# An earlier and more regular attention schedule beside the weight products, with four heads to a row half

## The chip, the cores and the metric

The kernel runs on one core of one Trainium2 chip. What counts is the device time of one execution, in microseconds. TensorE (PE) multiplies, with PEld its weight loads; VectorE (DVE), ScalarE (ACT) and GpSimd (POOL) do the elementwise work; SP, the sync engine, issues most DMAs. Each engine works through its own instructions in the order in which they were written, and waits on semaphores where an operand or a buffer is not there.

## The reference

Chunked attention over 4 batches, 8 heads, 768 positions of 64 values: each chunk of 32 queries sees 8 memory keys and the 56 keys around it (16 to the left, 32 own, 8 to the right). Its output, 3072 tokens of 512 values, goes through two gated layers:

```
scores = scale * q_c @ k_full.T ; a = softmax(scores) ; out_c = a @ v_full
x = ((x @ w1) * (x @ w2)) @ w3 @ w_out          # widths 1024, 1024, 512
y = ((x @ w_a) * (x @ w_b)) @ moe2_w_out        # widths 1536, 512
```

## The kernel before

**Weights' phase.** Since `w3 @ w_out` does not depend on the tokens, the kernel multiplies those two first (L548 to L583): two halves of 32 products of 128x512 in full fp32, eight steps of the inner sum for each of four PSUM banks. Products 1 to 24 of a half go step by step over the four banks, then each bank gets its steps 7 and 8 together. After a bank's last step `w_evict` (L543) copies it out with ACT and takes the rest with DVE; the second half needs the banks of the first. In the trace a product is two MATMUL instructions with the output `wps`.

**Weights.** They come as 64-bit floats. `w_load` (L339) issues a tile from SP if one of its buffers is free; `w_scale` (L355) passes it twice through ACT, `w_bits` (L364) sums on DVE. `w_tick` (L393) moves this pipe by one stage per tile and then calls `w_load` until no buffer is free. The plan has 12 tiles of 1 MB for the weights' phase (`w3a`, `w3b`, together `raw2` and `w_f`), then 16 of 0.5 MB for the first layer (`w12`, `raw64`), which take two ticks more (L403, L397) to become a high and a low half. The calls of `w_tick` in the phase are placed by hand.

**Attention.** It is cut into 16 units of 192 tokens with all eight heads (two groups of 96 queries). Each has stages: `a_k` and `a_q` load keys and queries, `a_keys` copies the keys into windows on DVE, `a_scores` multiplies on PE (`sc`), `a_max` and `a_exp` (16 activations, four of them in each of four stages) make exponentials, `a_norm` divides (DVE sums, POOL products, two stages), `a_trans` transposes on PE (`pt`), `a_pt` copies with ACT (`p`), `a_v` loads values, `a_pv` multiplies on PE (`xp`), `a_x` splits the result into the high and low part of the tokens' `xt`. `BASE` (L269) gives a unit's first slot, the table at L279 the slot of each stage behind it; `attn_slot` (L302) runs the next slot. Raw keys, queries, windows, values, `sc`, and the PSUM tile shared by `pt` and `xp` have one buffer each. Three units fill the first tile of 512 tokens.

**First layer.** For each of six tiles of 512 tokens, `ab_step` does for eight `m` a product A and B of 12 fp32r matmuls each (`psA`, `psB`, L595), then 96 matmuls `psY` with the product of the weights' phase. After each such half `between` (L620) calls `w_tick` while there are tiles in the pipe, and as many slots as bring the attention evenly to `NEED` (L299), the slot by which a token tile's units must be done. `xt` of tile 0 needs units 0 to 2. After six tiles the second layer runs with seven products per block (`seven`, L825); the change does not touch it.

Of the kernel before, what the change touches and what calls it, by code (L numbers as in the profile page):

```python
# [13 lines left out]
P = 128  # L14
# [31 lines left out]
def tile_attention_moe(  # L46
# [44 lines left out]


    ks, qs, scs, soft, pts, p2s, xps = ({} for _ in range(7))
    v = att.tile([P, NE * 2, NC, 2 * D], F32, tag="v", bufs=1, name="v")
    kw = att.tile([P, NH, NC, KEYS], F32, tag="kw", bufs=1, name="kw")
    xt = {}

# [6 lines left out]
    def rows(r):  # L104
        return slice(D * r, D * r + D)

    def new_batch(u):
        return NE * u % NG == 0

    def a_k(u):  # L110
        if u >= NA:
            return
        k = ks[u] = att.tile([P, NE * 2, 2 * KW], F32, tag="kraw", bufs=1, name="kraw")
        for r in range(2):
            src = kt[2 * NE * u : 2 * NE * u + 2 * NE, 0:D, 2 * r : 2 * r + 2, :]
            nc.sync.dma_start(out=k[rows(r)], in_=src.rearrange("a d h k -> d a (h k)"))

    def a_q(u):
        if u >= NA:
            return  # L120
        q = qs[u] = att.tile([P, NE * 2, 2 * GQ], F32, tag="q", bufs=1, name="q")
        for r in range(2):
            src = qt[2 * NE * u : 2 * NE * u + 2 * NE, :, 2 * r : 2 * r + 2, :]
            nc.sync.dma_start(out=q[rows(r)], in_=src.rearrange("a d h q -> d a (h q)"))

    def a_v(u):
        if u >= NA:
            return
        for r in range(2):
            src = vw[2 * NE * u : 2 * NE * u + 2 * NE, :, 2 * D * r : 2 * D * r + 2 * D]  # L130
            src = src.rearrange("a k d -> k a d")
            for c in range(NC):
                k0 = NMEM + CHUNK * c
                if new_batch(u):
                    nc.sync.dma_start(out=v[D * r : D * r + NMEM, :, c, :], in_=src[0:NMEM])
                nc.sync.dma_start(
                    out=v[D * r + NMEM : D * r + D, :, c, :], in_=src[k0 : k0 + KEYS - NMEM]
                )

    def a_keys(u):  # L140
        if u >= NA:
            return
        k = ks.pop(u).rearrange("p a (h k) -> p (a h) k", h=2)
        p, a, e = k.ap
        win = bass.AP(
            k.tensor, k.offset + NMEM * e[0], [p, a, [CHUNK * e[0], NC], [e[0], KEYS - NMEM]]
        )
        nc.vector.tensor_copy(kw[:, :, :, NMEM:], win)
        if new_batch(u):
            nc.vector.tensor_copy(  # L150
                kw[:, :, :, 0:NMEM], k[:, :, None, 0:NMEM].to_broadcast([P, NH, NC, NMEM])
            )

    def a_scores(u):
        q = qs.pop(u).rearrange("p a (h c q) -> p (a h) c q", h=2, c=NC)
# [75 lines left out]
    def a_pv(u):  # L231
        p2 = p2s.pop(u)
        xp = psa.tile([P, 2, 512], F32, tag="px", name="xp")
        xp = xps[u] = xp[:, :, : 2 * NE * GQ].rearrange("p r (a t) -> p a r t", a=2)
        for e in range(NE):
            for a in range(2):
                for c in range(NC):
                    q0 = CHUNK * c
                    for i in range(2):
                        for r in range(2):  # L240
                            h = r ^ i
                            mm(
                                xp[rows(h), a, r, GQ * e + q0 : GQ * e + q0 + CHUNK],
                                v[rows(r), 2 * e + a, c, rows(h)],
                                p2[rows(r), e, 2 * a + h, q0 : q0 + CHUNK],
                                True,
                                True,
                            )

    def a_x(u):  # L250
        xp = xps.pop(u)
        n = NE * GQ
        t0 = n * u
        cuts = [t0, t0 + n]
        if t0 // TT != (t0 + n - 1) // TT:
            cuts.insert(1, (t0 + n - 1) // TT * TT)
        parts = []
        for c0, c1 in zip(cuts, cuts[1:]):
            ti = c0 // TT
            if ti not in xt:  # L260
                xt[ti] = xpool.tile([P, 2, KD, TT], F32R, tag="xt", name="xt")
            x = xt[ti].rearrange("p l (a r) t -> p l a r t", a=2)
# [12 lines left out]

    for u in range(NA):
        early = u < UA
        t = 6 if early else 5
        for s, stage_of in (  # L279
            (t, a_trans),  # L280
            (t + early, a_pt),
            (t + 1 + early, a_pv),
            (t + 1 + early, lambda u: a_v(u + 1)),
            (0, a_scores),
            (1, a_max),
            (2, a_norm(0)),
            (3, a_norm(1)),
            (1, a_exp(0)),
            (1, a_exp(1)),
            (2, a_exp(2)),  # L290
            (2, a_exp(3)),
            (t + 2 + early, a_x),
            (1, lambda u: a_q(u + 1)),
        ):
# [4 lines left out]
    NEED = [BASE[-(-TT * (i + 1) // (NE * GQ)) - 1] + 8 + 2 * (i == 0) for i in range(NT1)]  # L299
    acount = [0]  # L300

    def attn_slot(n=1):  # L302
# [17 lines left out]
    NW0 = max(i for i, x in enumerate(plan) if x[0] == "w3b") + 1  # L320
    wraw = []
    nload = [0]

    turn = {tag: [0, 0] for tag in BUFS}
    live = {tag: [0, 0] for tag in BUFS}
# [224 lines left out]
    for half in range(2):  # L550
        banks = [psd.tile([P, 512], F32, tag="d", name="wps") for _ in range(4)]
        for k, m in order:
            mm(
                banks[m],
                w3k[8 * half + k].bitcast(F32)[:, P * m : P * m + P],
                wo_f[k].bitcast(F32),
                k == 0,
                k == 7,
            )
            if k < 6 and m % 2 == 0 or k == 6:  # L560
                continue

            if k == 7 and m > 0:
                w_evict(half, m - 1)
            if half == 0:
                if m == 1 and k < 6:
                    w_tick()
                if (k, m) == (1, 3):
                    a_k(0)
                    a_q(0)  # L570
                if (k, m) == (4, 3):
                    a_keys(0)
                    a_v(0)
                    a_k(1)
                if k == 7 and m > 0:
                    attn_slot()
                if k == 7 and m % 2 == 1:
                    w_tick()
            else:
                attn_slot()  # L580
                if m == 3 or k == 7 and m == 1:
                    w_tick()
        w_evict(half, 3)  # L583
    del pairs["f"]
# [425 lines left out]
```

## Time and profile before

| | |
|---|---|
| median of 3 runs | 1090.26 us (1089.99 to 1092.81) |
| the profiled execution's own time | 1093.22 us |
| its span, first to last instruction | 1091.4 us |
| PE busy in the span | 1065.6 us (98%) |
| ACT, DVE, POOL busy | 441.0, 457.1, 235.0 us |
| mean granted TensorE clock | 0.99 of full speed |

Times in the trace are microseconds from the span's start. A timeline row merges like instructions that follow each other on an engine; the bracket is the idle time ahead of it and what ended it. PE's busy time contains time at a lower clock.

### The profile page before, as it was taken

The page shows a single profiled execution, that of the slowest core. Times are in us where ns is not written, and L with a number is a line of the kernel's source. Part 1 is how long each engine was busy: PE and PEld are TensorE (multiplying, and loading weights), DVE is VectorE, ACT ScalarE, POOL GpSimd, SP SyncE. Part 2 cuts the span into 40 slices and gives each one's busy share as a digit, 9 for nine tenths or more (in the row PEclk, how much of TensorE's full clock was granted, in tenths as well). Part 3 has the DMA queues.
Part 4 walks back from the last instruction along what each step waited for, and adds up shares of the span by engine and source line. Part 5 has one row for each costly group of instructions (what it writes and reads, how often), then busy time and mean ns, then how long its engine had stood idle before and what let it go on. Part 6 is the DMA issues. An engine that isn't in the chain of part 4 may idle for free.

```text
span 1091.4 us, 18538 instructions
## 1 busy us (share of the span) xinstructions
PE 1065.6 (98%) x7442; PEld 848.0 (78%) x7442; DVE 457.1 (42%) x751; ACT 441.0 (40%) x1153; POOL 235.0 (22%) x228
## 2 busy tenths in 40 slices
PE   9688999999999999999999999999999999999998
PEld 3245778888888788888878888888888888888886
DVE  5547853454444445436553443442223243222320
ACT  6656864445545535435343333232222232222220
POOL 0110230221312212202122233104222301322210
PEclk9889999999999999999999999999999999999999
DMA  9868566345464473347545455514433442443311
GB/s 331 256 143 212 158 149 188 101 132 159 128 172 142 141 190 124 103 146 260 192 156 192 174 193 197 183 63 179 159 135 135 158 160 106 161 176 136 135 39 38
DMA packets 82693, 172.03 MB, mean 158 GB/s; under 512 B 7344, under 2 KB 46000, under 8 KB 76720
## 3 DMA queue, kind: packets, MB, share of 16 engines
q1 hardware_dynamic: 72032, 104.75, 32.3%
q0 software_dynamic: 10368, 66.06, 16.6%
q8 instruction: 58, 0.95, 0.4%
q14 instruction: 27, 0.22, 0.1%
q10 hardware_dynamic: 208, 0.04, 0.0%
HBM read 137.27 MB, written 33.55 MB: 157 GB/s over the span
## 4 chain that ended last, share of the span: by engine, by line
PE 83%; ACT 2%; DVE 1%; DMA 1%; POOL 1%; issue 0%; ACTq 0%; DVEq 0%
PE ps L796 31%; PE ops L90 18%; PE psY L90 12%; PE psB L90 10%; PE psA L90 9%; PE xp L90 2%; ACT t L195 1%; PE sc L90 1%; DMA wc<-co 1%; PE pt L223 1%; POOL g L615 0%; POOL t L212 0%; DVE dec L367 0%; DVE mx L186 0%; DVE x L102 0%
## 5 line engine op out<-in xcount | busy, mean ns | idle before, releaser
L796 PE MATMUL ps<-x,w 128*128 128x512 f32 x1512 | 348.9, 389 | 0.3 <-ACT tmp L808 0.3
L796 PEld LDWEIGHTS ps<-x,w 128*128 128x128 f32 x1512 | 283.4, 188 | 60.5 <-ACT tmp L808 1.4
L813 DVE TENSOR_TENSOR tmp<-ps,tmp 128x512 f32<-128x512 f32 x108 | 74.6, 690 | 261.0 <-PE ps L796 231.0
L90 PE MATMUL psA<-xt,w 128*128 128x512 f32 x576 | 140.6, 393 | 0.0
L90 PE MATMUL psB<-xt,w 128*128 128x512 f32 x576 | 140.0, 392 | 0.0
L615 POOL TENSOR_TENSOR g<-gv,g 128x512 fp32r<-128x512 f32 x48 | 66.9, 1394 | 320.4 <-ACT g L614 293.3
L90 PE MATMUL psY<-g,wo 128*128 128x512 f32 x576 | 135.6, 392 | 0.0
L808 ACT ACTIVATE tmp<-ps 128x512 f32<-128x512 f32 x108 | 64.6, 599 | 157.8 <-PE ps L796 151.2
L90 PEld LDWEIGHTS psA<-xt,w 128*128 128x128 f32 x576 | 107.2, 188 | 23.1 <-ACT raw L362 0.5
L90 PEld LDWEIGHTS psB<-xt,w 128*128 128x128 f32 x576 | 107.2, 188 | 22.5
L90 PEld LDWEIGHTS psY<-g,wo 128*128 128x128 f32 x576 | 107.1, 188 | 22.4
L680 POOL DMA_DIRECT2D w<-wc x72 | 39.7, 552 | 373.8 <-PE ps L796 373.6
L90 PE MATMUL ops<-wo,g 128*128 128x512 f32 x504 | 118.6, 389 | 0.0
L90 PEld LDWEIGHTS ops<-wo,g 128*128 128x128 f32 x504 | 94.6, 188 | 19.7
L819 ACT ACTIVATE g<-tmp 128x512 fp32r<-128x512 f32 x66 | 40.7, 633 | 139.9 <-DVE tmp L818 139.9
L820 POOL TENSOR_TENSOR g<-tmp,g 128x512 fp32r<-128x512 f32 x66 | 84.1, 1293 | 20.4 <-ACT g L819 19.4
L195 ACT ACTIVATE t<-sc,mx 96x64 f32<-96x64 f32 x256 | 75.7, 321 | 23.5 <-DVE mx L187 23.5
L90 PE MATMUL wps<-w_f 128*128 128x512 f32 x128 | 65.9, 665 | 9.2 <-DVE wo L546 5.6
L90 PE MATMUL ops<-fo,g 128*128 128x512 f32 x288 | 68.2, 389 | 0.0
L90 PEld LDWEIGHTS ops<-fo,g 128*128 128x128 f32 x288 | 54.1, 188 | 11.2
L613 DVE TENSOR_TENSOR gv<-psB,av 128x512 f32<-128x512 f32 x48 | 33.1, 689 | 67.1 <-PE psB L90 56.1
L212 POOL TENSOR_TENSOR t<-t,sm 96x512 f32<-96x512 f32 x32 | 36.8, 1150 | 103.0 <-DVE sm L211 80.0
(65 smaller groups left out, 904.7 us busy)
## 6 DMA issues: line engine op xcount, KB each, us to landing
w<-wc POOLq DMA_DIRECT2D x36, 1024.0 KB, 6.9
w<-wc POOLq DMA_DIRECT2D x36, 768.0 KB, 5.0
wc<-co SPq DMA_DIRECT2D x84, 256.0 KB
raw<-in_wab SPq DMA_DIRECT2D x24, 512.0 KB
v<-in_vw SPq DMA_DIRECT2D x96, 112.0 KB
kraw<-in_kt SPq DMA_DIRECT2D x32, 256.0 KB
raw<-in_w SPq DMA_DIRECT2D x16, 512.0 KB
raw<-in_w3a SPq DMA_DIRECT2D x6, 1024.0 KB
```

The costliest lines, as they stand in the source:

```text
L90: nc.tensor.matmul(o, lhsT=l, rhs=r, start=first, stop=last)
L195: nc.scalar.activation(t[:, a, r, :], sc[:, r, a, :], AF.Exp, bias=mx[:, r, a : a + 1], scale=SCALE, accum_out=sm[:, a, r : r + 1],)
L212: nc.gpsimd.tensor_tensor(t, t, sm[:, :, :, None].to_broadcast([GQ, 4, 2, KEYS]), ALU.mult)
L223: nc.tensor.transpose(pt[:, a // 4, a % 4, :], t[:, a].rearrange("p r k -> p (r k)"), id_sb)
L613: nc.vector.tensor_tensor(gv, psB[:, :TT], av, ALU.mult)
L615: nc.gpsimd.tensor_tensor(g2[:, 1, :], gv, g2[:, 0, :].bitcast(F32), ALU.subtract)
L680: nc.gpsimd.dma_start(out=t[:, c0:c1].bitcast(F32), in_=src[:, c0:c1])
L796: nc.tensor.matmul(ps, lhsT=w[:, i, a, k, :], rhs=xs[i][:, b, k, :], start=first and n == 0, stop=n == 5, skip_group_check=not first,)
L808: nc.scalar.activation(z, ps, AF.Copy)
L813: nc.vector.tensor_tensor(z, ps, y, ALU.add)
L819: nc.scalar.activation(g2[:, 0, :], z, AF.Copy)
L820: nc.gpsimd.tensor_tensor(g2[:, 1, :], z, g2[:, 0, :].bitcast(F32), ALU.subtract)
```

## The change

Four things, in one edit.

1. The layout of a unit in the two row halves. Before, rows 0 to 63 held heads 0 and 1 of each four, rows 64 to 127 heads 2 and 3. Now each row half holds all four heads of one group of four. So a run of keys in memory is 2 KB instead of 1 KB, of queries 1536 bytes instead of 768, of values 1 KB instead of 512, and the three windows of values come in one DMA.
2. The slots: `BASE` starts 0, 7, 14, 23, 30, 36 and then goes on by 7; the first six units have one slot more between scores and transposes and one more before the probabilities' copy; unit 0 has all its exponentials in slot 1; queries of the next unit are loaded in the slot of the scores, raw keys of the next with the copy of the keys.
3. The weights' phase: `a_k(0)` and `a_q(0)` come after the third tick, the first slot after product 18; there are 24 slots instead of 19 (with unit 3's scores in the last), and the ticks stand elsewhere (19 before and now).
4. `w_load` issues no tile of the first layer until product 42 (`bound`).

```diff
-    v = att.tile([P, NE * 2, NC, 2 * D], F32, tag="v", bufs=1, name="v")
+    v = att.tile([P, NE, NC, 4 * D], F32, tag="v", bufs=1, name="v")
...
+    def group(src, u, r):
+        return src[2 * NE * u : 2 * NE * u + 2 * NE].rearrange("(e r) x h y -> r x e (h y)", r=2)[r]
...
-            src = kt[2 * NE * u : 2 * NE * u + 2 * NE, 0:D, 2 * r : 2 * r + 2, :]
-            nc.sync.dma_start(out=k[rows(r)], in_=src.rearrange("a d h k -> d a (h k)"))
+            nc.sync.dma_start(out=k[rows(r)], in_=group(kt[:, 0:D], u, r))
...
+                win = bass.AP(
+                    src.tensor,
+                    src.offset + NMEM * kd[0],
+                    [[kd[0], KEYS - NMEM], [CHUNK * kd[0], NC], x],
                 )
+                nc.sync.dma_start(out=v[D * r + NMEM : D * r + D, e, :, :], in_=win)
...
-    BASE = [0, 5, 9]
-    BASE += [BASE[-1] + 10 + 7 * i for i in range(NA - UA)]
+    BASE = [0, 7, 14, 23, 30, 36]
+    NX = len(BASE)
+    BASE += [BASE[-1] + 7 * i for i in range(1, NA - NX + 1)]
...
-        early = u < UA
-        t = 6 if early else 5
+        x = int(u < NX)
+        t = 5 + 2 * x
         for s, stage_of in (
-            (t, a_trans),
-            (t + early, a_pt),
-            (t + 1 + early, a_pv),
-            (t + 1 + early, lambda u: a_v(u + 1)),
+            (5 + x, a_trans),
+            (t, a_pt),
+            (t + 2, a_x),
+            (t + 1, a_pv),
+            (t + 1, lambda u: a_v(u + 1)),
             (0, a_scores),
+            (0, lambda u: a_q(u + 1)),
...
-            (2, a_exp(2)),
-            (2, a_exp(3)),
+            (1 + (u > 0), a_exp(2)),
+            (1 + (u > 0), a_exp(3)),
...
-            at(BASE[u] - 2, (a_keys, u))
-            at(BASE[u] - 1, (a_k, u + 1))
+            at(BASE[u] - 2, (a_keys, u), (a_k, u + 1))
+    at(0, (a_v, 0))
...
-        if i < len(wsrc):
+        if i < bound[0]:
...
+    a_k(0)
+    a_q(0)
...
+            g = 2 * k + m // 2 if k < 6 else 12 + m
             if half == 0:
...
+                if g == 7:
                     a_keys(0)
                     a_k(1)
+                if g >= 8:
                     attn_slot()
+                if g in (0, 2, 4, 6, 8, 9, 14):
                     w_tick()
             else:
                 attn_slot()
+                if g == 4:
+                    bound[0] = len(wsrc)
+                if g in (1, 3, 4, 5, 6, 9, 10, 11, 12):
                     w_tick()
```

PE in the weights' phase, before (each `sc`, `pt`, `xp` row is one unit's):

```order
L90 MATMUL wps<-w_f 128x512 x28
L90 MATMUL sc<-kw,q 32x64 x48
L90 MATMUL wps<-w_f 128x512 x10
L90 MATMUL sc<-kw,q 32x64 x48
L90 MATMUL wps<-w_f 128x512 x2
L223 MATMUL pt<-id_sb,t 128x96 x8
L90 MATMUL wps<-w_f 128x512 x4
L90 MATMUL xp<-p_451,v 64x32 x48
```

PE in the same phase with the change, and its end at the first `psA`:

```order
L90 MATMUL wps<-w_f 128x512 x18
L90 MATMUL sc<-kw,q 32x64 x48
L90 MATMUL wps<-w_f 128x512 x12
L227 MATMUL pt<-id_sb,t 128x96 x8
L90 MATMUL wps<-w_f 128x512 x2
L90 MATMUL sc<-kw,q 32x64 x48
L90 MATMUL wps<-w_f 128x512 x2
L90 MATMUL xp<-p_354,v 64x32 x48
...
L90 MATMUL wps<-w_f 128x512 x2
L90 MATMUL sc<-kw,q 32x64 x48
L90 MATMUL psA<-xt,w_693 128x512 x12
```

The first scores moved from product 28 to 18, the first transposes and probability-by-value products forward by 10 and 8 products, and unit 3's scores to the front of `psA`.

ACT from the seventh weight tile on, before (`raw` rows scale a tile, `wo` rows evict a bank, `t` rows are exponentials):

```order
L361 ACTIVATE raw_183<-raw_183 128x1024
L362 ACTIVATE raw_183<-raw_183 128x1024
L545 ACTIVATE wo<-wps 128x512
L361 ACTIVATE raw_193<-raw_193 128x1024
L362 ACTIVATE raw_193<-raw_193 128x1024
L545 ACTIVATE wo<-wps 128x512
L195 ACTIVATE t,sm<-sc,mx 96x64 x8
L545 ACTIVATE wo<-wps 128x512
L195 ACTIVATE t,sm<-sc,mx 96x64 x8
```

ACT with the change (`raw_172` is the eighth tile, `raw_183` the ninth, `raw_277` the eleventh, `raw_523` the first of the first layer):

```order
L370 ACTIVATE raw_172<-raw_172 128x1024
L371 ACTIVATE raw_172<-raw_172 128x1024
L199 ACTIVATE t,sm<-sc,mx 96x64 x16
L370 ACTIVATE raw_183<-raw_183 128x1024
L371 ACTIVATE raw_183<-raw_183 128x1024
L557 ACTIVATE wo<-wps 128x512 x2
...
L370 ACTIVATE raw_277<-raw_277 128x1024
L371 ACTIVATE raw_277<-raw_277 128x1024
...
L370 ACTIVATE raw_523<-raw_523 128x512
L371 ACTIVATE raw_523<-raw_523 128x512
L233 ACTIVATE p_544<-pt 128x768
```

All 16 exponentials of unit 0 stand ahead of the evictions now, and the copy of unit 1's probabilities (`p_544`) stands behind the first tile of the first layer.

SP's queue with the change, from the sixth tile (`raw_143`) and, lower, from unit 2's keys on:

```order
L355 DMA raw_143<-in_w3a 128x2048
L118 DMA kraw<-in_kt 64x2x512 x2
L125 DMA q<-in_qt 64x2x384 x2
L355 DMA raw_162<-in_w3a 128x2048
L355 DMA raw_172<-in_w3a 128x2048
...
L118 DMA kraw<-in_kt 64x2x512 x2
L125 DMA q<-in_qt 64x2x384 x2
L142 DMA v<-in_vw 56x3x256 x4
L118 DMA kraw<-in_kt 64x2x512 x2
L355 DMA raw_523<-in_w 128x1024
```

Before, the first keys and queries stood behind the eighth tile, and the first-layer tiles ahead of unit 1's queries.

## Rows read from the trace of the kernel before

**Rows 1.** The page, part 2: tenths in 40 slices of the span, granted clock below.

```profile
PE   9688999999999999999999999999999999999998
PEclk9889999999999999999999999999999999999999
```

**Rows 2.** Windows, first weight product to first psA: busy us by engine, clock, DMA share, GB/s.

```profile
8.58:99.14 90.56, 75.75 (x729) 36.02 (x729) 49.10 (x74) 57.49 (x153) 7.67 (x6) 0.89 0.81 229
```

**Rows 3.** Timeline of PE, weights' phase: start, us, what, [idle before, releaser].

```profile
8.58 21.98 PE L90 MATMUL wps<-w_f 128*128 128x512 f32 x50
34.11 4.54 PE L90 MATMUL wps<-w_f 128*128 128x512 f32 x6 [3.55 <-DVE w_f L367]
38.58 1.19 PE L90 MATMUL sc<-kw,q 64*32 64x64 f32 x96
...
47.25 1.37 PE L90 MATMUL wps<-w_f 128*128 128x512 f32 x2 [2.13 <-DVE wo L546]
52.10 5.49 PE L90 MATMUL wps<-w_f 128*128 128x512 f32 x6 [3.49 <-DVE wo L546]
59.96 0.27 PE L90 MATMUL sc<-kw,q 64*32 64x64 f32 x2 [2.37 <-DMA q<-in_qt]
...
77.58 0.82 PE L223 MATMUL pt<-id_sb,t 96*128 96x96 f32 x8
...
82.88 1.60 PE L90 MATMUL xp<-p,v 64*64 64x32 f32 x96 [1.00 <-ACT p L229]
...
94.83 1.59 PE L90 MATMUL xp<-p,v 64*64 64x32 f32 x78 [0.54 <-DMA v<-in_vw]
```

**Rows 4.** Timeline of DVE, weights' phase.

```profile
31.06 0.86 DVE L148 COPY kw<-kraw 128x1344 f32<-128x1344 f32 x1 [4.32 <-DMA kraw<-in_kt]
...
32.83 1.23 DVE L367 CUSTOM_DVE_ANT_0 w_f<-raw,w_f 128x2048 uint16<-128x2048 uint16 x1
...
46.50 0.69 DVE L546 TENSOR_TENSOR wo<-wps,wo 128x512 fp32r<-128x512 f32 x1 [3.06 <-ACT wo L545]
```

**Rows 5.** Timeline of ACT, weights' phase.

```profile
28.59 1.15 ACT L361 ACTIVATE raw<-raw 128x1024 f32<-128x1024 f32 x1 [3.10 <-DMA raw<-in_w3a]
...
43.53 0.31 ACT L195 ACTIVATE t<-sc,mx 96x64 f32<-96x64 f32 x1 [2.59 <-DVE mx L187]
...
45.87 0.60 ACT L545 ACTIVATE wo<-wps 128x512 fp32r<-128x512 f32 x1
...
86.23 0.68 ACT L361 ACTIVATE raw<-raw 128x512 f32<-128x512 f32 x1 [0.33 <-DMA raw<-in_w]
```

**Rows 6.** Timeline of SP's queue: start and length of DMA issues.

```profile
11.75 6.74 SPq L346 DMA_DIRECT2D raw<-in_w3a  x3
18.54 1.48 SPq L116 DMA_DIRECT2D kraw<-in_kt  x2
...
47.78 1.74 SPq L124 DMA_DIRECT2D q<-in_qt  x2
...
78.47 6.97 SPq L346 DMA_DIRECT2D raw<-in_w  x2
```

**Rows 7.** Windows of 2 us, columns as in rows 2.

```profile
14.00:16.00 2.00, 1.92 (x5) 0.68 (x4) 1.43 (x3) 1.71 (x3) 0.00 (x0) 1.00 1.02 430
24.00:26.00 2.00, 2.00 (x6) 0.91 (x5) 1.18 (x2) 1.49 (x2) 0.00 (x0) 1.00 1.00 158
34.00:36.00 2.00, 1.89 (x3) 0.86 (x4) 0.06 (x1) 0.70 (x1) 0.00 (x0) 0.59 1.05 438
82.00:84.00 2.00, 1.12 (x76) 1.12 (x80) 1.77 (x4) 1.93 (x6) 1.29 (x1) 1.00 0.86 220
```

**Rows 8.** Timeline of PE in the first token tile: the rows with idle time.

```profile
122.13 1.60 PE L90 MATMUL xp<-p,v 64*64 64x32 f32 x96 [1.23 <-ACT p L229]
143.85 0.55 PE L223 MATMUL pt<-id_sb,t 96*128 96x96 f32 x4 [1.87 <-POOL t L212]
170.57 1.60 PE L90 MATMUL xp<-p,v 64*64 64x32 f32 x96 [0.50 <-ACT p L229]
```

More of the change, by code (lines that the diff above doesn't have):

```diff
@@ L112, in a_k @@
             return
-        k = ks[u] = att.tile([P, NE * 2, 2 * KW], F32, tag="kraw", bufs=1, name="kraw")
+        k = ks[u] = att.tile([P, NE, 4 * KW], F32, tag="kraw", bufs=1, name="kraw")
         for r in range(2):
-            src = kt[2 * NE * u : 2 * NE * u + 2 * NE, 0:D, 2 * r : 2 * r + 2, :]
-            nc.sync.dma_start(out=k[rows(r)], in_=src.rearrange("a d h k -> d a (h k)"))
+            nc.sync.dma_start(out=k[rows(r)], in_=group(kt[:, 0:D], u, r))
     def a_q(u):
@@ L120, in a_q @@
             return
-        q = qs[u] = att.tile([P, NE * 2, 2 * GQ], F32, tag="q", bufs=1, name="q")
+        q = qs[u] = att.tile([P, NE, 4 * GQ], F32, tag="q", bufs=1, name="q")
         for r in range(2):
-            src = qt[2 * NE * u : 2 * NE * u + 2 * NE, :, 2 * r : 2 * r + 2, :]
-            nc.sync.dma_start(out=q[rows(r)], in_=src.rearrange("a d h q -> d a (h q)"))
+            nc.sync.dma_start(out=q[rows(r)], in_=group(qt, u, r))
     def a_v(u):
@@ L129, in a_v @@
         for r in range(2):
[L130 to L133, printed above, removed]
+            for e in range(NE):
+                src = vw[2 * NE * u + 2 * e + r]
+                kd, x = src.ap
                 if new_batch(u):
-                    nc.sync.dma_start(out=v[D * r : D * r + NMEM, :, c, :], in_=src[0:NMEM])
-                nc.sync.dma_start(
-                    out=v[D * r + NMEM : D * r + D, :, c, :], in_=src[k0 : k0 + KEYS - NMEM]
+                    for c in range(NC):
+                        nc.sync.dma_start(out=v[D * r : D * r + NMEM, e, c, :], in_=src[0:NMEM])
+                win = bass.AP(
+                    src.tensor,
+                    src.offset + NMEM * kd[0],
+                    [[kd[0], KEYS - NMEM], [CHUNK * kd[0], NC], x],
                 )
+                nc.sync.dma_start(out=v[D * r + NMEM : D * r + D, e, :, :], in_=win)
     def a_keys(u):
@@ L142, in a_keys @@
             return
-        k = ks.pop(u).rearrange("p a (h k) -> p (a h) k", h=2)
+        k = ks.pop(u).rearrange("p e (h k) -> p (e h) k", h=4)
         p, a, e = k.ap
@@ L154, in a_scores @@
     def a_scores(u):
-        q = qs.pop(u).rearrange("p a (h c q) -> p (a h) c q", h=2, c=NC)
+        q = qs.pop(u).rearrange("p e (h c q) -> p (e h) c q", h=4, c=NC)
         sc = psa.tile([GQ, 2, 512], F32, tag="sc", name="sc")
@@ L233, in a_pv @@
         xp = psa.tile([P, 2, 512], F32, tag="px", name="xp")
-        xp = xps[u] = xp[:, :, : 2 * NE * GQ].rearrange("p r (a t) -> p a r t", a=2)
+        xp = xps[u] = xp[:, :, : 2 * NE * GQ].rearrange("p r (a t) -> p r a t", a=2)
         for e in range(NE):
@@ L242, in a_pv @@
                             mm(
-                                xp[rows(h), a, r, GQ * e + q0 : GQ * e + q0 + CHUNK],
-                                v[rows(r), 2 * e + a, c, rows(h)],
+                                xp[rows(h), r, a, GQ * e + q0 : GQ * e + q0 + CHUNK],
+                                v[rows(r), e, c, rows(2 * a + h)],
                                 p2[rows(r), e, 2 * a + h, q0 : q0 + CHUNK],
@@ L261, in a_x @@
                 xt[ti] = xpool.tile([P, 2, KD, TT], F32R, tag="xt", name="xt")
-            x = xt[ti].rearrange("p l (a r) t -> p l a r t", a=2)
+            x = xt[ti].rearrange("p l (r a) t -> p l r a t", r=2)
             parts.append((xp[..., c0 - t0 : c1 - t0], x[..., c0 - TT * ti : c1 - TT * ti]))
@@ L289, in tile_attention_moe @@
             (1, a_exp(1)),
-            (2, a_exp(2)),
-            (2, a_exp(3)),
-            (t + 2 + early, a_x),
-            (1, lambda u: a_q(u + 1)),
+            (1 + (u > 0), a_exp(2)),
+            (1 + (u > 0), a_exp(3)),
         ):
@@ L296, in tile_attention_moe @@
         if u > 0:
-            at(BASE[u] - 2, (a_keys, u))
-            at(BASE[u] - 1, (a_k, u + 1))
-    NEED = [BASE[-(-TT * (i + 1) // (NE * GQ)) - 1] + 8 + 2 * (i == 0) for i in range(NT1)]
+            at(BASE[u] - 2, (a_keys, u), (a_k, u + 1))
+    at(0, (a_v, 0))
+    NEED = []
+    for i in range(NT1):
+        u = -(-TT * (i + 1) // (NE * GQ)) - 1
+        NEED.append(BASE[u] + 8 + 2 * (u < NX))
     acount = [0]
@@ L322, in tile_attention_moe @@
     nload = [0]
+    bound = [NW0]
     turn = {tag: [0, 0] for tag in BUFS}
@@ L564, in tile_attention_moe @@
                 w_evict(half, m - 1)
+            g = 2 * k + m // 2 if k < 6 else 12 + m
             if half == 0:
[L566 to L571, printed above, removed]
+                if g == 7:
                     a_keys(0)
-                    a_v(0)
                     a_k(1)
-                if k == 7 and m > 0:
+                if g >= 8:
                     attn_slot()
-                if k == 7 and m % 2 == 1:
+                if g in (0, 2, 4, 6, 8, 9, 14):
                     w_tick()
@@ L580, in tile_attention_moe @@
                 attn_slot()
-                if m == 3 or k == 7 and m == 1:
+                if g == 4:
+                    bound[0] = len(wsrc)
+                if g in (1, 3, 4, 5, 6, 9, 10, 11, 12):
                     w_tick()
```

## The prediction

> **What bounds the kernel now.** I read the page first. PE is busy nearly the whole span; the only slices with room, and the only ones below full clock, are the first four of forty, the first 109 us [rows 1]. So the change, which works there, is judged by PE alone: when the weights' phase ends, and what PE waits for in it.
>
> The windows view gives the size. From the first weight product at 8.58 to the first psA product at 99.14, PE is busy 75.75 of 90.56 us [rows 2], so idle 14.81. PE's timeline says what the busy time should be: 25 products (two instructions each) take 21.98 us, 0.88 each; one unit's scores take 1.19, its transposes 0.82, its probability-by-value products 1.60 [rows 3]. 64 products and three of each make 56.3 + 10.8 = 67.1. The other 8.6 us of busy time is half clock: after the idle 3.55 us three products take 4.54 us in place of 2.64, and the granted clock there is 0.59, near the lower of its two levels (1.2 of 2.4 GHz) [rows 3, 7]. The phase thus loses 23.4 us to idleness and to the slow clock behind it.
>
> The same timeline names the waits, and the other engines' timelines say who was late:
> - 3.55 us before the 26th product [rows 3], for the eighth weight tile. ACT started to scale it at 28.59, but DVE stood at the key copy until 31.06, waiting 4.32 us for raw keys, and only then finished the tile's sum at 34.06 [rows 4, 5].
> - 2.13 and 3.49 us [rows 3], for PSUM banks. Their evictions stand on ACT behind exponentials: the first starts at 43.53, the third eviction at 45.87, and DVE's part at 46.50 [rows 4, 5].
> - 2.37 us for unit 1's queries [rows 3], issued at 47.78 behind four weight tiles [rows 6]; 1.00 us for a probability copy; 0.40, 0.80 and 0.54 us for values (the last has its row) [rows 3].
> Three more are in the first token tile: 1.23, 1.87 and 0.50 us [rows 8]. Behind those PE has next to no gaps.
>
> **The change part by part.** PE's work is unchanged in sum; unit 3's scores (1.19) move ahead of psA. So the old end to compare with is 99.14 + 1.19 = 100.3, and without idleness or slow clock the new one would be 8.58 + 67.1 + 1.19 = 76.9.
>
> First scores after product 18. PE is there at 8.58 + 18 x 0.88 = 24.4. Keys and queries were issued at 18.54 and copied 12.5 us later [rows 4, 6]. They now stand behind the sixth tile: SP issues three tiles from 11.75, the later two only when a buffer comes free [rows 6], so the keys leave at about 12.3. With the same 12.5 us they are there at 24.8; on DVE the copies (0.86, about 0.25) follow the sixth tile's sum. I take 26.3 for the scores: idle 1.9, between 0 (sum and keys both early) and 4 (keys and tile share the queue to the end).
>
> Tiles seven and eight. 0.92 MB of keys and queries are now ahead of them. At the 430 GB/s of the weights alone that is 2.1 us, at the 158 of the stretch with keys and queries in flight 5.8 [rows 7]. Runs of 1 KB and 768 B become 2 KB and 1.5 KB, so I take 2.5. Against that the eighth tile no longer waits on DVE for keys. It is usable at about 34, as before; PE wants it after 25 products and the scores, 26.3 + 1.2 + 6.2 = 33.7. Idle 0.5 in place of 3.55, between 0 and 3. The Trainium skill ("DMA: Bandwidth & Descriptors", Specifications) gives 512 B as the least transfer for line rate; by it the longer runs would buy nothing. The fall to 158 in this trace speaks against it, though it does not separate the keys from what ran beside them.
>
> Evictions. All 16 exponentials of unit 0 now stand ahead of the first eviction, when no bank is due, so 2.13 + 3.49 goes. What is late next: ACT begins them after the eighth tile's scaling, near 33; eight take 2.34 (43.53 to 45.87) [rows 5], so they end near 37.7 and POOL's second normalisation near 40. The transposes come when PE has done 30 products, about 39, and wait for it as unit 4's do now (1.87 [rows 8]): I take 0.8. Product 33 needs the ninth tile's sum, on DVE behind the eviction and unit 1's key copy, near 44.6: 1.4. Product 41 needs the tenth's, behind unit 0's x: 0.5. Together 2.7, between 1 and 6.
>
> Unit 1's queries now follow the first scores, some 14 us early: the 2.37 goes. The values of units 1 and 2 also have over 10 us: the 1.74 goes.
>
> Weights of the first layer held back. They are issued after product 42, behind raw keys that wait for DVE to copy the keys before. ACT starts the eleventh tile at 53; scaling (2.2), sum (1.9), key copy (0.9), two key issues (1.3) and one tile issue give 59.8. ACT must scale that tile before it copies unit 1's probabilities, which PE wants at 62.7. A tile issued at 78.47 was reached at 86.23 [rows 5, 6]: with those 7.8 us, 2 of scaling and copying make 69.6, idle 6.9; below it is nothing, if other work delays PE. The old tile had values, keys, a tile and queries ahead of it, this one keys alone; I take 4.5 us, idle 3.6. The same order on ACT puts four more tiles ahead of unit 2's copy: 0.9, between 0 and 4.
>
> Sum of idle: 1.9 + 0.5 + 2.7 + 3.6 + 0.9 = 9.6, for 14.81. Slow clock: a wait of 3.55 cost 1.9 more, while one of 1.00 at 82.88 left the clock at 1.00 [rows 3, 7]. Two waits here are long; I take 3, between 0 and 5.6 (the old ratio 8.6 / 14.81 of the idle time). The phase ends at 76.9 + 9.6 + 3 = 89.5, 10.8 earlier.
>
> First token tile. Units 3 to 5 get one slot between scores and transposes and one before the copy is used; a slot is at least one 12-product half, 2.7 us, more than 1.23, 1.87 or 0.50. Held-back weights make ACT fuller there, so I take 2.5 of 3.6, between 0 and 3.6. From the third token tile on the order on PE is as before: nothing.
>
> SP's extra small value loads for a new batch (six more) and fewer large ones stand where SP waits anyway: nothing; with that cover gone, under 2 us.
>
> Total 10.8 + 2.5 = 13.3. The profiled execution took 1093.22 (span 1091.4), 3 us above the median of 1090.26; it would come to 1079.9, and the median to 1077.0.
>
> **The rivals.**
> 1. Few waits are left: keys early, the held-back tile lands in time. Idle 4, no slow clock: the phase ends at 81, 6 to 8 us better, about 1069. For it: both bounds at nothing. Against it: ACT and DVE run in order and each of the waits has a named cause.
> 2. Runs of 512 B and more gain nothing. The eighth tile is then 3.3 later than taken, idle up by some 3: 1080. For it: the page named above. Against it: 158 beside 430 GB/s.
> 3. Clock and chains eat more: the idle time is fragmented but PE stays slow as long as it did (8.6) and waits reach 13 of their upper bounds: the phase ends at 98, and with 1.5 later that is 1086 to 1089. For it: after 0.40, 0.80 and 0.54 us of waits the old phase ended slowly too.
> 4. Slower: the held-back weights arrive too late for the first token tile. Sixteen tiles through three buffers from 60 us; the last is due near 137. A tile that takes 7.8 to land, 2.3 to be summed and up to 2.8 to its turn costs 12.9 / 3 = 4.3 each, and the last is there at 129. With the 12.5 us that the raw keys took, it is 17.6 / 3 = 5.9 each, 154: 17 us late, more than all that is gained, about 1097 with slow clock. It decides from 5.6 each on. Against it: the old fifth tile was issued at 78.47, the new one between 70 and 76.
> That the change does not do what it says is excluded: the order of instructions shows the scores after product 18 and unit 3's before psA.
>
> **How the numbers follow.** Forecast (1071 to 1083, rival 2's 1080 within it but priced apart): 0.50; rival 1: 0.13; rival 2: 0.13; rival 3: 0.18, half of it within 0.3%; rival 4: 0.06. 0.3%, or 3.3 us, is about what a measurement here can tell from no change: 1087.0 to 1093.5. Faster 0.50 + 0.13 + 0.13 + 0.09 = 0.85, same 0.09, slower 0.06. The range leaves out 0.05 of rival 1 below 1068 and, above 1087, 0.15.
>
> **What would show it.** The first scores near 26, with idle time for the key copy; no PE wait on evictions over 1.5 us; a wait of unit 1's probability-by-value products for ACT, with ACT idle for a DMA of the first held-back tile; psA at 87 to 92; no gap at units 3 to 5. It would be wrong if PE waits for the seventh or eighth tile by more than 3 us, if psA starts after 95, or if products of the first token tile wait for weights.

## The result, and the profile after

The changed kernel takes 1081.13 us in the median of four runs (1080.40 to 1082.25), the old one beside it 1091.35 (1089.99 to 1092.81): a ratio of 0.9907, 95% interval 0.9888 to 0.9926, 10.2 us faster. That is inside the range and 4 us above the forecast. The profiled execution took 1080.40 us, its span is 1078.6 us, the mean granted clock 0.998. Its own time is 12.8 us below that of the old profile, which was a long one of its kernel.

The page, part 2, answers to [rows 1]: no slice is below nine tenths of the clock now, and room is left in some of the first five slices.

```profile
PE   9889899999999999999999999999999999999998
PEclk9999999999999999999999999999999999999999
```

The window from the first weight product to the first psA product, columns as in [rows 2]:

```profile
8.30:89.83 81.53, 70.50 (x825) 35.20 (x825) 47.40 (x73) 56.60 (x153) 6.78 (x6) 0.98 0.84 261
```

PE is idle for 81.53 - 70.50 = 11.03 us (14.81 before). With unit 3's scores the busy time at full clock would be 67.1 + 1.19 = 68.3, so 70.50 - 68.3 = 2.2 are on top of that (8.6 before), the prediction's measure of the slow clock. By the rows, 1.6 of the 2.2 are slow clock, in the two rows behind the longest wait (2.32 for 1.60 and 9.71 for 8.85); the rest is spread over rows at full clock. Both sums fell; the busy time gave back more than the waits.

PE's timeline in that window, against [rows 3], shows every wait of the 11.03 us:

```profile
8.30 7.26 PE L90 MATMUL wps<-w_f 128*128 128x512 f32 x16
15.77 8.85 PE L90 MATMUL wps<-w_f 128*128 128x512 f32 x20 [0.21 <-DVE w_f L376]
25.31 1.28 PE L90 MATMUL sc<-kw,q 64*32 64x64 f32 x96 [0.69 <-DVE kw L154]
...
34.76 4.56 PE L90 MATMUL wps<-w_f 128*128 128x512 f32 x10 [1.97 <-DVE w_f L376]
...
44.17 1.98 PE L90 MATMUL wps<-w_f 128*128 128x512 f32 x4 [1.24 <-DVE w_f L376]
...
53.77 3.70 PE L90 MATMUL wps<-w_f 128*128 128x512 f32 x8 [0.67 <-DVE w_f L376]
...
66.72 2.32 PE L90 MATMUL xp<-p,v 64*64 64x32 f32 x96 [3.80 <-ACT p L233]
...
85.25 1.60 PE L90 MATMUL xp<-p,v 64*64 64x32 f32 x96 [2.45 <-ACT p L233]
...
89.83 3.04 PE L90 MATMUL psA<-xt,w 128*128 128x512 f32 x12
```

The waits on evictions, queries and values are gone. What is left is weight sums that come late on DVE (1.97, 1.24, 0.67) and two probability copies that come late on ACT (3.80, 2.45). Only the longest shows in the clock, after full clock up to 66:

```profile
68.00:70.00 2.00, 2.00 (x42) 1.42 (x39) 0.04 (x1) 1.84 (x13) 0.00 (x0) 0.50 0.89 288
```

The eighth tile (1.97), on ACT and then on DVE:

```profile
27.50 1.14 ACT L370 ACTIVATE raw<-raw 128x1024 f32<-128x1024 f32 x1 [4.44 <-DMA raw<-in_w3a]
...
29.98 1.18 ACT L370 ACTIVATE raw<-raw 128x1024 f32<-128x1024 f32 x1 [0.27 <-DMA raw<-in_w3a]
```

```profile
31.32 1.22 DVE L190 TENSOR_REDUCE mx<-sc 96x16 f32<-96x1024 f32 x1
...
33.48 1.22 DVE L376 CUSTOM_DVE_ANT_0 w_f<-raw,w_f 128x2048 uint16<-128x2048 uint16 x1
```

ACT begins the eighth tile at 29.98 and passes it twice, yet its sum ends at 33.48 + 1.22 = 34.70, as unit 0's score maximum stands ahead of it on DVE. In [rows 4] it was the key copy.

The late copy (3.80), on ACT: 8.30 us idle for a tile of the first layer, then the copy that PE wants.

```profile
64.76 0.65 ACT L370 ACTIVATE raw<-raw 128x512 f32<-128x512 f32 x1 [8.30 <-DMA raw<-in_w]
65.32 0.66 ACT L371 ACTIVATE raw<-raw 128x512 uint32<-128x512 uint32 x1
65.88 0.79 ACT L233 ACTIVATE p<-pt 128x768 f32<-128x768 f32 x1
```

In the first token tile PE's rows with idle time are these, against [rows 8]; they sum to 3.10 us where 3.60 were.

```profile
115.07 1.60 PE L90 MATMUL xp<-p,v 64*64 64x32 f32 x96 [1.05 <-ACT p L233]
...
130.14 1.20 PE L90 MATMUL psA<-xt,w 128*128 128x512 f32 x4 [0.52 <-DVE w L406]
...
133.18 1.28 PE L90 MATMUL sc<-kw,q 64*32 64x64 f32 x96 [1.18 <-DVE kw L152]
...
152.66 0.73 PE L90 MATMUL psY<-g,wo 128*128 128x512 f32 x2 [0.35 <-POOL g L624]
```

The account of the profiled executions: psA begins 100.3 - 89.83 = 10.5 us earlier. The first token tile gives 0.5. Two waits for POOL in the second and third token tile of the old kernel, 0.22 at 294.76 and 0.86 at 372.72, are gone: 1.1. In the third token tile a like row of `psY`, before and then with the change, says what is won by then:

```profile
395.92 3.01 PE L90 MATMUL psY<-g,wo 128*128 128x512 f32 x12
```

```profile
383.25 3.01 PE L90 MATMUL psY<-g,wo 128*128 128x512 f32 x12
```

That is 12.7; 0.6 of it has no row, and hardly anything is won later (12.8 in the whole span). By the medians the gain is smaller, 10.2, because the profiled execution of the old kernel was a long one.

### The profile page after: what moved, and what is told of

It is laid out like the page before. It is cut to its first block, busy times and chain, and to the rows that moved or that the text cites. A ratio compares the mean times of both kernels' runs of the same rounds, so it can differ in the third digit from the quotient of the medians.

```text
span 1078.6 us, 18525 instructions
## 1 busy us (share of the span) xinstructions
PE 1058.0 (98%) x7442; PEld 846.1 (78%) x7442; DVE 456.6 (42%) x751; ACT 441.4 (41%) x1153; POOL 231.1 (21%) x228
## 4 chain that ended last, share of the span: by engine, by line
PE 85%; DVE 1%; ACT 1%; DMA 1%; issue 0%; SPq 0%; POOL 0%; ACTq 0%; DVEq 0%; POOLq 0%
PE ps L805 31%; PE ops L90 18%; PE psY L90 12%; PE psA L90 10%; PE psB L90 10%; PE xp L90 2%; PE sc L90 1%; PE pt L227 1%; DMA raw<-in_wab 1%; DMA raw<-in_w 1%; ACT t L199 0%; DVE dec L375 0%; SPq L125 0%; DVE x L102 0%; DVE tmp L659 0%
## 5 line engine op out<-in xcount | busy, mean ns | idle before, releaser
L624 POOL TENSOR_TENSOR g<-gv,g 128x512 fp32r<-128x512 f32 x48 | 63.5, 1322 | 273.3 <-ACT g L623 273.1
L90 PE MATMUL wps<-w_f 128*128 128x512 f32 x128 | 59.2, 609 | 4.2 <-DVE w_f L376 4.1
L370 ACT ACTIVATE raw<-raw 128x512 f32<-128x512 f32 (+1 forms) x66 | 49.0, 742 | 28.0 <-DMA raw<-in_w 12.8
```

The source lines that it names most:

```text
L90: nc.tensor.matmul(o, lhsT=l, rhs=r, start=first, stop=last)
L370: nc.scalar.activation(h, h, AF.Prelu, scale=2.0**-112, alpha=2.0**32)
L624: nc.gpsimd.tensor_tensor(g2[:, 1, :], gv, g2[:, 0, :].bitcast(F32), ALU.subtract)
```

## The experiments

Each was run beside the kernel before, and ratios are to that. The versions of one group shared a chip and its runs of before.

### Layout alone, schedule alone

`e1_layout` is the kernel before with part 1 of the change alone, `e2_schedule` the changed kernel with the old layout (parts 2 to 4).

```diff
 e1_layout
-            src = kt[2 * NE * u : 2 * NE * u + 2 * NE, 0:D, 2 * r : 2 * r + 2, :]
-            nc.sync.dma_start(out=k[rows(r)], in_=src.rearrange("a d h k -> d a (h k)"))
+            nc.sync.dma_start(out=k[rows(r)], in_=group(kt[:, 0:D], u, r))
...
 e2_schedule
-            nc.sync.dma_start(out=k[rows(r)], in_=group(kt[:, 0:D], u, r))
+            src = kt[2 * NE * u : 2 * NE * u + 2 * NE, 0:D, 2 * r : 2 * r + 2, :]
+            nc.sync.dma_start(out=k[rows(r)], in_=src.rearrange("a d h k -> d a (h k)"))
...
```

> The layout alone (four heads to a row half, longer runs), with the old slots, ticks and loads. My theory: the old waits are set by the order of work, so they stay (the eviction waits of 2.13 and 3.49 us, the query wait), and only the wait for the eighth weight tile shrinks a little; the time is 0 to 3 us below the kernel before. Rival: the longer runs carry the gain; 6 us or more below the kernel before, with the eviction waits gone.

> The changed slots, ticks and loads with the old layout and its short runs. My theory: first keys and queries take longer again (some 160 to 210 GB/s while they are in flight, not 235 to 250), so the wait ahead of the eighth weight tile grows from 1.97 to 3 to 4 us and the time is 1 to 3 us above the changed kernel. Rival (runs of 512 B and more are all alike): within 1 us of the changed kernel. Second rival (layout carries the gain): back to within 3 us of the kernel before.

Layout alone: 1091.35 us (10 runs), ratio 0.999 [0.9974, 1.0006]. The old waits are there in PE's timeline, for the eighth tile and for the evictions:

```profile
31.98 2.84 PE L90 MATMUL wps<-w_f 128*128 128x512 f32 x6 [1.50 <-DVE w_f L371]
...
44.59 2.08 PE L90 MATMUL wps<-w_f 128*128 128x512 f32 x2 [3.29 <-DVE wo L550]
...
49.51 5.20 PE L90 MATMUL wps<-w_f 128*128 128x512 f32 x6 [2.85 <-DVE wo L550]
```

As expected, the one for the eighth tile is shorter (1.50 instead of 3.55): ACT reaches that tile at 26.98 instead of 28.59, and from 24 to 30 the queues move 241 instead of 203 GB/s. That is one execution of each kernel, the old one a long one; the eviction waits together are no shorter (3.29 + 2.85 against 2.13 + 3.49), and the interval leaves the layout at most 2.8 us.

Schedule alone: 1081.61 us (4 runs), ratio 0.9895 [0.987, 0.9921], with waits like those of the changed kernel (1.77 for the eighth tile, 3.43 and 1.26 for the copies; 1.97, 3.80 and 2.45 there). The 3 to 4 us expected for the eighth tile did not come. So the schedule has the whole gain, as far as these runs can tell. The windows in which keys and queries are in flight ahead of tile seven, of the changed kernel and then of the schedule alone:

```profile
18.00:20.00 2.00, 2.00 (x6) 0.95 (x5) 1.36 (x3) 1.53 (x2) 0.00 (x0) 1.00 1.05 250
20.00:22.00 2.00, 2.00 (x6) 0.88 (x5) 0.79 (x1) 1.13 (x2) 0.00 (x0) 1.00 1.13 235
22.00:24.00 2.00, 2.00 (x6) 0.84 (x5) 1.60 (x2) 1.06 (x2) 0.00 (x0) 1.00 1.08 239
```

```profile
18.00:20.00 2.00, 2.00 (x6) 0.80 (x6) 1.35 (x3) 1.34 (x2) 0.00 (x0) 1.00 1.08 236
20.00:22.00 2.00, 2.00 (x6) 0.93 (x5) 0.81 (x2) 1.38 (x2) 0.00 (x0) 1.00 1.15 212
22.00:24.00 2.00, 2.00 (x6) 0.76 (x4) 1.65 (x3) 0.81 (x1) 0.00 (x0) 1.00 1.12 272
```

Over the three windows runs of 2 KB and 1.5 KB move no faster (250, 235, 239 GB/s) than runs of 1 KB and 768 B (236, 212, 272), and with the short runs ACT reaches tile seven no later (27.05 against 27.50). The DMA engines are busy the whole time in both (shares above 1), at little more than half of the 415 GB/s that the weights alone reach in the window from 16 to 18. The Trainium skill ("DMA: Bandwidth & Descriptors", Specifications) puts the least transfer for line rate at 512 B; both layouts are above it for keys and queries, and the trace agrees: in this schedule nothing is left to gain from the length. What makes these loads slow is something else.

### Is it the queue or the row half?

`e7_queues` issues unit 0's keys and queries of rows 64 to 127 from ACT, so that the halves go side by side and past SP.

```diff
-            nc.sync.dma_start(out=k[rows(r)], in_=group(kt[:, 0:D], u, r))
+            eng = nc.scalar if (u, r) == (0, 1) else nc.sync
+            eng.dma_start(out=k[rows(r)], in_=group(kt[:, 0:D], u, r))
...
```

> The changed kernel with unit 0's keys and queries of rows 64 to 127 issued by ACT, beside those of rows 0 to 63 from SP. Theory (a load into one half of the rows reaches half the bandwidth, and two loads in one queue follow each other): with both halves in flight the rate between 18 and 24 us rises from 235 to 250 to over 350 GB/s, ACT reaches the seventh tile 1.5 to 2.5 us before 27.50, and the wait of 1.97 shrinks to under 1; the time is 0.5 to 2.5 us below the changed kernel. Rival (something else about these loads, whatever half they go to): the rate stays under 290 and the seventh tile is scaled at 27 or later.

1080.12 us (6 runs), ratio 0.9905 [0.989, 0.9921]. The windows from 16 to 26 move 348, 285, 291, 201 and 378 GB/s, and ACT reaches tile seven at 27.67, no earlier than 27.50. The wait for the eighth tile did fall to 0.85, but the first scores come later (26.58, after a wait of 1.90), so nothing is won by it. That the two halves only wait for each other in one queue is thus not the reason. Whether it is that each load fills 64 rows and not 128 is untested: no run loads all rows with one DMA. Why keys and queries keep the queues busy for so long stays open.

### The weights of the first layer: not held, held one tick less

```diff
 e3_nohold
-    bound = [NW0]
+    bound = [len(wsrc)]
...
 e4_hold3
-                if g == 4:
+                if g == 3:
                     bound[0] = len(wsrc)
```

> The changed kernel with the first layer's weights not held back (issued as buffers come free, so right behind the twelfth tile). My theory: ACT finds the first of these tiles landed, the wait of 3.80 us ahead of unit 1's probability-by-value products goes with the slow clock behind it (about 0.9), nothing else is late by more than 1 us; 3 to 5 us below the changed kernel. Rival: the three tiles delay unit 2's keys and queries or unit 1's values, and waits of 3 us or more appear there; the time is the same as or above the changed kernel.

> The changed kernel with the held-back weights released one tick earlier (after product 40 instead of 42), so that SP issues them ahead of unit 3's raw keys and not behind that wait for DVE. My theory: issued near 55 instead of 58.7, the first lands by 61, the wait of 3.80 falls under 1 us, the slow clock stretch at 67 to 71 goes, and the pipe is one tile further, so 2.45 and 0.52 shrink; 4 to 6 us below the changed kernel. Rival: the next thing in ACT's order is late instead, and the time is within 2 us of the changed kernel.

Not held: 1081.59 us (4 runs), ratio 0.9906 [0.9877, 0.9934]. The 3.80 is gone from PE's timeline; two waits are new (2.01 and 1.02), and unit 2's copy costs 3.29 instead of 2.45:

```profile
61.50 0.27 PE L90 MATMUL sc<-kw,q 64*32 64x64 f32 x2 [2.01 <-DMA q<-in_qt]
...
68.02 8.74 PE L90 MATMUL wps<-w_f 128*128 128x512 f32 x20 [1.02 <-issue]
...
84.18 2.34 PE L90 MATMUL xp<-p,v 64*64 64x32 f32 x96 [3.29 <-ACT p L233]
```

Now the tiles are ahead of unit 2's queries on SP. Part 4 of the change trades a wait for queries against one for the copy and is worth nothing that can be measured here.

Released one tick earlier: 1082.36 us (4 runs), ratio 0.9903 [0.9876, 0.9929]. The wait is still 3.77, because a tick earlier puts two tiles ahead of the copy on ACT, and the first took 8.3 us from its issue at 54.10:

```profile
62.36 0.67 ACT L370 ACTIVATE raw<-raw 128x512 f32<-128x512 f32 x1 [6.35 <-DMA raw<-in_w]
...
64.37 0.65 ACT L370 ACTIVATE raw<-raw 128x512 f32<-128x512 f32 x1 [0.80 <-DMA raw<-in_w]
...
65.49 0.79 ACT L233 ACTIVATE p<-pt 128x768 f32<-128x768 f32 x1
```

The place of the copy in ACT's order decides, not the issue of the tile.

### The copy ahead of the late tile

For units 0 to 2 the probability copy goes into the slot of the transposes; that slot comes ahead of the tick.

```diff
-            (t, a_pt),
+            (t - (u < 3), a_pt),
```

> The changed kernel with the copy of the probabilities of units 0 to 2 in the slot of their transposes, so ahead of the first-layer tile that ACT scales next. My theory (ACT's order is what PE waits for): the waits of 3.80 and 2.45 us ahead of units 1's and 2's probability-by-value products fall under 0.5 us each and the slow clock near 67 to 71 goes; psA starts 4 to 7 us earlier, the time is 3 to 6 us below the changed kernel. Rival (the late tile itself is the bound): DVE still waits for it ahead of unit 2's maximum, the wait moves to unit 2's transposes or to psA, and the time is within 1.5 us of the changed kernel.

> Both of the two changes before together. My theory: their gains add, 4 to 8 us below the changed kernel, near 1075. Rival: the next late thing (the ninth tile's sum, DVE ahead of unit 2's maximum) takes most of it, and the time is within 2 us of the better of the two alone.

`e5_copyfirst`: 1078.03 us (1077.35 to 1079.06, 5 runs), ratio 0.9887 [0.9872, 0.9902]: every run is below those of the changed kernel, and the median is the lowest of all versions. The intervals of the two ratios overlap, though: 0.9887 against 0.9907 is some 2 us, where 3 to 6 were expected. `e8_both` adds the other queue: 1078.33 us (6 runs), ratio 0.9892 [0.9876, 0.9907], nothing on top. In the first, PE's products of unit 1 wait for nothing, but the weight product behind them does:

```profile
62.95 1.60 PE L90 MATMUL xp<-p,v 64*64 64x32 f32 x96
67.53 10.35 PE L90 MATMUL wps<-w_f 128*128 128x512 f32 x20 [2.98 <-issue]
```

"issue" says that the profile shows no releaser, and in the program that product waits on no semaphore either: its weights were summed by 59.4. The 3.80 of the changed kernel had covered this wait; taking the cover away let psA begin 2.0 us earlier (87.79), not the 3.80 and the slow clock behind it.

### What PE waits for there

Two readings were put to the test: PE's own instructions come late, or PE's queue has a limit that shows behind 96 small matmuls. In the window from 64 to 66 of `e5_copyfirst`, in the middle of that stretch, the DMA queues move 408 GB/s of weights, and one packet of another kind (queue, kind: packets, MB, share of 16 engines):

```profile
q8 instruction: 1, 0.02, 3.1%
```

The next two versions release the first-layer weights after product 48 and after product 52, with as many ticks as before. The order of work on PE is the same.

```diff
 e9_hold7 (and e10_hold9: 9, with ticks at 1, 3, 4, 9 to 14)
-                if g == 4:
+                if g == 7:
                     bound[0] = len(wsrc)
-                if g in (1, 3, 4, 5, 6, 9, 10, 11, 12):
+                if g in (1, 3, 4, 7, 8, 9, 10, 11, 12):
                     w_tick()
```

> The version with unit 1's copy ahead of the late tile, with the first-layer weights released after product 48 instead of 42 (three ticks later). Question: what is the 2.98 us that PE waits after unit 1's probability products without a releaser? PE's next instruction there has no semaphore to wait for in the program, so my theory is that PE's own instructions come late, their block (one packet of 16 KB on the instruction queue, landing at 64 to 66 us) standing behind the three 0.5 MB weight tiles that were issued at 58.8. With nothing but unit 2's queries in the queues from 60 to 63 the wait is then under 1.5 us, psA near 86, time 1075 to 1078. Rival: it has nothing to do with the DMA load (a limit in PE's queue after 96 small matmuls): wait 2.5 to 3.5 again. Either way the later weights may cost something in the first token tile: up to 2 us.

> The same with the release after product 52, some 67 us, when PE is past the place. Late-instructions theory: no wait without a releaser over 0.5 us there, psA 85 to 86. Rival (PE's queue): 2.5 to 3.5 us as before. For the slower side of my prediction (weights late for the first token tile): the first tiles are now issued near 67 instead of 58.8, so if that edge is near, PE waits for w tiles from 95 to 140 us, by 2 to 8 us in sum; if there is slack, under 1.5 us more than now.

PE's timeline of `e9_hold7`:

```profile
63.11 1.60 PE L90 MATMUL xp<-p,v 64*64 64x32 f32 x96
64.64 8.85 PE L90 MATMUL wps<-w_f 128*128 128x512 f32 x20
...
80.13 1.60 PE L90 MATMUL xp<-p,v 64*64 64x32 f32 x96 [2.51 <-ACT p L233]
...
115.76 0.53 PE L90 MATMUL xp<-p,v 64*64 64x32 f32 x18 [1.68 <-issue]
```

The wait is gone in both, with the same 96 small matmuls ahead: the rival, a limit of PE's queue behind them, falls. The instruction packet is in the window 60 to 62 now (it begins at 61.57, against 64.87 in `e5_copyfirst`), and 62 to 64 in `e10_hold9`, ahead of the weights. So when the weights are in flight decides about this wait. A wait of the same kind turns up at 115.76 (1.01 in the other), inside the 96 products of a later unit, which PE reaches at 112.72 here and, behind a wait for the copy, at 115.07 in the changed kernel; the DMA load is no higher there (242 and 230 GB/s from 112 to 114).

The traces say more about the first reading. PE's instructions up to such a wait, matmuls and weight loads, are the first two counts (x) of a window that begins with the span and ends in the wait (`e11_sumfirst`, `e5_copyfirst`, `e9_hold7`, `e6_nx3`):

```profile
0.00:52.20 52.20, 43.57 (x348) 19.26 (x348) 26.12 (x39) 33.36 (x78) 2.28 (x6) 0.97 0.88 298
0.00:67.50 67.50, 58.26 (x602) 27.55 (x603) 36.13 (x54) 42.96 (x103) 4.90 (x8) 1.00 0.90 284
0.00:115.73 115.73, 102.75 (x1112) 57.29 (x1112) 71.96 (x113) 80.34 (x217) 13.84 (x15) 1.00 0.80 243
0.00:119.28 119.28, 103.01 (x1112) 58.84 (x1112) 73.16 (x114) 83.00 (x221) 13.62 (x15) 0.97 0.79 239
```

All eight waits without a releaser in the versions' timelines stand behind one of three such counts: 696, 1205 (`e3_nohold`, `e5_copyfirst`, `e8_both` and the second of `e11_sumfirst`) and 2224 (`e9_hold7`, `e10_hold9`, `e6_nx3`). At 2224 PE is inside probability products in `e9_hold7` and inside scores in `e6_nx3`, so the place in its instruction stream decides and not the kind of work. And each of the eight ends 1.3 to 1.7 us after a packet of 16384 bytes of the instruction queue has ended: 65.85 and then 67.53 in `e5_copyfirst`, 50.90 and 52.23 in `e11_sumfirst`, 117.91 and 119.31 in `e6_nx3`. So PE waits there for its own instructions, as far as a trace can show it. That the weights in flight hold the packet up is inferred: no run moved the packet alone. The Trainium skill ("Runtime: NRT & Kernel Launch", Instruction fetch mechanics) says that an engine's instructions come in blocks of 16 KiB over a DMA queue of its own, and that the cost is mostly hidden. The packet has that size (0.02 MB); hidden the cost is not always here: 2.98 us beside 408 GB/s of data.

Times: 1079.60 us, 0.9891 [0.9875, 0.9908], and 1078.85 us, 0.9883 [0.9865, 0.9901] (4 runs each), not below `e5_copyfirst` by anything that can be measured; 1075 to 1078 were expected of the first. psA begins at 86.01 and 84.59 against 87.79 in `e5_copyfirst`, up to 3.2 us earlier, but the `psY` row in the third token tile at 382.21 and 382.22 against 381.50. The first token tile takes all of it back; two of its rows in `e10_hold9`:

```profile
84.59 0.50 PE L90 MATMUL psA<-xt,w 128*128 128x512 f32 x1 [1.63 <-ACT xt L99]
...
131.10 1.20 PE L90 MATMUL psA<-xt,w 128*128 128x512 f32 x4 [1.88 <-DVE w L406]
```

Waits for first-layer weights are 0.67, 0.46 and 1.88 there, 3.0 in sum, and 0.52 in the changed kernel. So the edge of the prediction's rival 4 (weights late for the first token tile) is near: a release some 9 us later (67.7 instead of 58.7 on SP) costs 2.5 us of it, not 17.

### The eighth tile's sum ahead of the maximum

On top of `e5_copyfirst`, DVE finishes the eighth tile before unit 0's score maximum.

```diff
+                if g == 9:
+                    i, r, tag = pipe[0].pop(0)
+                    w_sum(i, r)
+                    live[tag][int(tag == "raw2")] -= 1
                 if g >= 8:
                     attn_slot()
```

> The version with unit 1's copy ahead of the late tile, and on DVE the sum of the eighth weight tile ahead of unit 0's score maximum. Theory: the wait of 1.9 us for that tile falls to about 0.6 (the sum ends at 33.5 instead of 34.8), but the exponentials start 2 us later and POOL's second normalisation ends near 41: the transposes wait for it by 2 to 3 us. Sum about the same, time within 0.3% of the version without. Rival: the exponentials have slack and the 1.3 us is won, with the slow clock behind it perhaps 2.

1082.49 us (4 runs), ratio 0.9915 [0.9896, 0.9935], some 3 us worse by the ratios than without (the intervals just touch). In PE's timeline the tile's wait falls to 0.35, and the transposes wait for POOL in its place:

```profile
33.79 4.56 PE L90 MATMUL wps<-w_f 128*128 128x512 f32 x10 [0.35 <-DVE w_f L376]
...
39.73 0.55 PE L227 MATMUL pt<-id_sb,t 96*128 96x96 f32 x4 [1.38 <-POOL t L216]
42.06 0.55 PE L227 MATMUL pt<-id_sb,t 96*128 96x96 f32 x4 [1.78 <-POOL t L216]
...
52.23 0.65 PE L90 MATMUL xp<-p,v 64*64 64x32 f32 x26 [2.15 <-issue]
```

The waits on POOL came as the theory had them (1.38 + 1.78), but its sum did not: a further 2.15 us without a releaser was not expected, and the clock behind it is at 0.50 from 54 to 56. It stands at the first of the three counts above. At the second one PE waits 3.50. The order of the change looks like the better one.

### The extra slots of units 3 to 5

```diff
-    NX = len(BASE)
-    BASE += [BASE[-1] + 7 * i for i in range(1, NA - NX + 1)]
+    NX = 3
+    BASE += [BASE[-1] + 7 * i for i in range(1, NA - 5)]
```

> The changed kernel without the two extra slots of units 3 to 5. My theory: the extra slots were worth little, as the new waits in the first token tile (1.05, 0.52, 1.18, 0.35) come from the weights' pipe on ACT and DVE; without them waits of 1 to 2 us come back ahead of transposes or probability products, and the time is 0 to 2 us above the changed kernel. Rival (the slots cover a lot): waits of over 4 us in all, 3 us or more above the changed kernel.

1081.00 us (1079.06 to 1084.38, 4 runs), ratio 0.9916 [0.9894, 0.9938]: the same time as with them, within a spread that is wide here. The profiled execution is the longest of the four and differs already in the weights' phase, so its waits say little about the slots. With `e3_nohold` this leaves the gain to the earlier slots, loads and ticks of the weights' phase (parts 2 and 3 of the change), which no run takes apart.

## Why the prediction was right, and where its steps were not

**The sum.** Its own time was forecast at 1079.9 and measured at 1080.40; psA at 89.5 and 89.83. Of the 4.1 us between the median's 1077.0 and 1081.13, 3.7 come from one step: "3 us above the median" of before was carried over to the changed kernel. The changed kernel's profile is at the low end of its runs, not above them. A single execution's place among its runs belongs to that execution; the 3 us should have gone into the range. That the profile's time came out within 0.5 is in part luck: the first token tile gave 2.0 less than forecast, while 1.1 of waits that were left out and 0.6 without a row made most of it up.

**Idle 9.6, slow clock 3.** Measured 11.03 and 2.2. Inside the idle time errors cancelled, which is luck too. The evictions' successors were 1.24 and 0.67 on the ninth and tenth tiles' sums (1.4 and 0.5 forecast) and nothing on POOL (0.8). Unit 1's copy cost 3.80 (3.6), behind the tile that was named. The first scores took 0.69 and 0.21 for 1.9: the keys were copied at 24.23.

**"Idle 0.5" for the eighth tile** was 1.97. The chain behind it was incomplete: the sum was counted when the tile was scaled, and what else stands on DVE ahead of it, unit 0's maximum, was not. The sum came 0.7 later than forecast (34.70 for 34), and PE was there 0.9 earlier (32.79 for 33.7), as its first scores had waited less. `e11_sumfirst` shows that the maximum makes most of the wait (0.35 without it ahead, 1.89 with it in `e5_copyfirst`), and that the wait can't be had for free.

**The longer runs.** "The fall to 158 in this trace speaks against it" was the wrong reading, and the delay taken, 2.5, was too small: tile seven was reached 4.2 us later than in the old kernel (27.50 and 23.30). Layout and schedule apart show that run length buys nothing that can be measured, as rival 2 has it. The late tile costs no more because the eighth follows it by 2.5 us. Rival 2's 1080 lies nearer to 1081.13 than the forecast. Its premise held, but not its price: it had the eighth tile 3.3 later than forecast, and it was 0.7.

**Unit 2's copy**, 0.9 forecast, 2.45 measured, stands behind tiles on ACT as said; the term was too small.

**The first token tile**: 2.5 forecast, 0.5 measured. The copies' two waits shrank to one of 1.05 and the transposes' 1.87 went, but a key copy (1.18), a weight sum (0.52) and POOL (0.35) came up. The two later waits (1.1) were left out as "nothing". Two of the prediction's own signs speak against it here: it named no gap at units 3 to 5, and there are 1.05 and 1.18; and it would be wrong "if products of the first token tile wait for weights", and one does, for 0.52. The other signs came: first scores at 25.31 behind the key copy, no wait on evictions, unit 1's copy behind the named tile, psA at 89.83.

**The rivals.** Rival 1 needed a phase end of 81, rival 3 of 98. Rival 4's mechanism exists, but the changed kernel has 0.52 of it.

## What to carry to other kernels

When waits are taken out of an in-order engine, look for the instruction that the late one now stands behind, on the engine that feeds it: both long waits left here were copies queued behind a load that nobody needed yet. Moving the consumer's instruction won some 2 us, moving the load alone moved the wait. A part of a change that sounds like bandwidth should be run alone; here it was worth nothing that could be measured, and the order of the work everything.

## What the runs showed of the hardware

- While keys and queries are loaded, the DMA engines are fully busy at 201 to 291 GB/s (18 to 24 us), where weight tiles alone run at 415, in either run length and from one or two queues; why is open.
- A 0.5 MB tile needed 6 us and more from issue to use where unit loads were ahead of it (58.70 to 64.76; 54.10 to 62.36).
- PE can stop for 1.0 to 3.2 us and, in one version, 3.50 us (at 73.83 in `e11_sumfirst`), with nothing to wait for in the program. The stops stand at fixed places of its instruction stream (696, 1205 and 2224 instructions) and end 1.3 to 1.7 us after a 16384-byte packet of the instruction queue.
- In the changed kernel the clock stayed at 1.00 after waits of 1.97 and 2.45 us, and fell to 0.50 after 3.80. Elsewhere it fell to 0.50 after 2.98 (`e5_copyfirst`), 2.42 (84.81 in `e7_queues`), 2.15 (`e11_sumfirst`) and 1.88 (34.62 in `e10_hold9`), so the length of a wait alone does not tell.
